# Second pair of a two-phase kernel: subtractions and operand loads placed elsewhere in the chains, part of them on another engine

## The chip, the cores and the metric

One core of one Trainium2 chip runs the whole program. The metric is device time in microseconds (us) of one execution, and a kernel's time is the median of its runs. The engines are named as the profile names them: PE (TensorE, matmuls) with PEld (its weight loads), DVE (VectorE), ACT (ScalarE), POOL (GpSimd) and SP (SyncE, which issues all DMAs here). Each engine works through its own instructions strictly in the order written; semaphores tie the engines together.

## The reference

```python
def reference(**kwargs):          # attention, then two MLPs, 4608 tokens
    attn_out = _attn_ref(...)     # linear attention, 8 x 8 x 576 x 64
    x = ...                       # 4608 x 512
    x = _moe_ref(x, w_in, w_out)              # (h * cos(h)) @ w_out, h = x @ w_in
    return _moe2_ref(x, w1, w2, w3, w_out)

def _moe2_ref(x, w1, w2, w3, w_out):          # w1, w2: 512 x 1024, w3: 1024 x 1024
    a = x @ w1
    b = x @ w2
    h = a * b @ w3
    return (h @ w_out).astype(np.float32)
```

The change touches only the last function, here called the second pair.

## The kernel before

The program first does the attention and the first MLP, and writes the second MLP's input x2, transposed, to device memory. It also multiplies w3 by w_out once (the tensor w_c), so that the second pair is a, b = x2 w1, x2 w2 (phase one) and o = (a*b) w_c (phase two). Each product of fp32 matrices is done as three matmuls of a high and a low part: ACT copies the rounded high part (line 122), DVE or POOL subtracts it to get the low part (line 124). All three products use a recursive 2 x 2 scheme with seven products of sums of blocks in place of eight, so every operand is needed in seven combinations (0 to 6), which take further subtractions.

**Phase one** runs over twelve pairs (h, g): h is a half of w1 and w2, g one of six groups of 768 tokens. A pair has four chains (`Chain`, `at` = 0 to 3), and a chain has seven products of six matmuls of 384 columns. The order on PE is `open1` (product 1 into bank X, product 2 into bank Y), `close1` of the chain before (its product 4), `open2` (product 6 into X), `close2` of the chain before (its product 3), `open3` (product 5 into V, product 7 into X). Call these the slots 1 to 7 of a chain. By the table `PAIR` they read the token operands `xc` 0, 1, 6 (of the chain before), 4, 2 (of the chain before), 3 and 5. ACT copies X out three times per chain (line 1396) before PE may add to X again; chains with `at` 0 and 2 make a, those with 1 and 3 make b, and `done` multiplies (line 1447) and `quarter` (lines 1364 to 1372) makes four subtractions and additions per product a*b. The seven resulting combinations of a*b go to device memory (line 1345).

**The token operands** of the next group come from `xc_steps` (line 1301): one tile `x2r` (tag "x", a single buffer) is loaded by four DMAs; then seven ACT copies, seven low-part subtractions and four subtractions of blocks (lines 1319, 1321, 1322, 1328) make xc 0, 1, 4, 3, 5, 2, 6 in that order. Eight buffers of tag "xc" hold seven operands, so a new operand takes the place of one whose last product has been read. All eleven subtractions run on POOL, while POOL also makes `quarter` from the seventh pair on (line 1594). Where in the chains a step is written is set by tables in `second` (lines 1558 to 1588): (pair, chain, place), with places o1, c1, o2, c2, o3 after open1, close1, and so on. `w12_steps` (line 1165) and `wc_stages` (line 1274) are placed in the same way; `wc_stages` makes the operands `wq` of w_c in the last pairs, in two halves h, all its subtractions on POOL.

**Phase two** (`Out`) runs over eighteen pairs of 2 x 128 tokens: seven products of twelve matmuls of 256 columns each. Its left operands are the seven stored combinations of a*b, loaded by `load_left` in three DMAs (of 3, 3 and 1 combinations) and split by `split_left` on ACT and DVE. The loads of pair n+2 are written at the end of pair n, and pair n+1 is split during pair n.

Of the kernel before, what the change touches and what calls it, by code (L numbers as in the profile page):

```python
# [33 lines left out]
def kernel(  # L34
# [1418 lines left out]
    def load_left(n, i):  # L1453
        if n < len(PAIRS):
            g, s = PAIRS[n]
            k = len(COMBOS[i])
# [79 lines left out]
    def second(last_set):  # L1536
# [27 lines left out]
        for dp, i, at in (  # L1564
            (0, 0, ((0, 3, "o1"), (1, 0, "o3"), (1, 1, "o1"), (1, 1, "o2"), (1, 2, "o1"),
                    (1, 2, "c1"))),
            (0, 1, ((1, 3, "o1"), (2, 0, "o3"), (2, 1, "o1"), (2, 1, "o2"), (2, 1, "o3"),
                    (2, 2, "o1"))),
            (1, 0, ((2, 0, "o3"), (2, 2, "o2"), (2, 2, "o3"), (2, 3, "o1"), (2, 3, "o2"),
                    (2, 3, "o3"))),  # L1570
            (1, 1, ((2, 1, "o1"), (3, 0, "o1"), (3, 0, "o2"), (3, 0, "o3"), (3, 1, "o1"),
                    (3, 1, "o2"))),
# [12 lines left out]
        on((k, 3, "c1"), load_left, 0, 1)
        on((k, 3, "c1"), load_left, 0, 2)
        on((k, 3, "o3"), split_left, 0, 1)
        on((k, 3, "o3"), split_left, 0, 2)
# [316 lines left out]
```

## Time and profile before

| | us |
|---|---|
| median of 3 runs | 1472.31 (1470.74 to 1475.21) |
| the profiled execution | 1474.78 |
| its span, first to last instruction | 1473.0 |
| PE busy | 1418.3 (96%) |
| DVE busy | 947.5 (64%) |
| ACT busy | 718.5 (49%) |
| POOL busy | 641.1 (44%) |

The profile is one execution, 1.8 us longer than its span. A share of busy time is an average over stages; matmuls overlap, so a busy PE can still run slowly. What a stage loses is read from the starts of its matmuls: their number times the pace of an undisturbed stretch, against the time that passed. The granted clock of a stretch is given as a share of 2.4 GHz.

### The profile page before, as it was taken

How to read it: one execution, taken by the hardware profiler on the slowest of the kernel's cores; microseconds unless marked ns; L12 is line 12 of the kernel's file. 1: busy time of each engine (PE TensorE's matmuls, PEld its weight loads, DVE VectorE, ACT ScalarE, POOL GpSimd, SP SyncE). 2: the span in 40 equal slices, each digit the busy share in tenths (PEclk: the TensorE clock that was granted, in tenths of full speed). 3: DMA queues.
4: the chain of work that ended last, by engine and by line, in shares of the span. 5: the costliest groups of instructions: out<-in, count | busy, mean ns of one | idle time of the engine just before them, and what ended most of it. 6: DMA issues, size and time to landing. Idle time of an engine off the chain costs nothing.

```text
span 1473.0 us, 23476 instructions
## 1 busy us (share of the span) xinstructions
PE 1418.3 (96%) x8376; PEld 1246.3 (85%) x8376; DVE 947.5 (64%) x1500; ACT 718.5 (49%) x1365; POOL 641.1 (44%) x522
## 2 busy tenths in 40 slices
PE   7999999999999999999999999999999889899998
PEld 5877777777777889988888879999999889899998
DVE  5786566674878667888888675666653333555553
ACT  5665655555556555555555354433333233445453
POOL 1174664485554622122223197845665476600000
PEclk9999999999999999999999999999999999999999
DMA  9385996797689988999999844445424243566654
GB/s 340 124 283 143 317 287 208 246 324 243 197 301 342 351 326 310 323 322 359 345 358 368 290 167 139 144 129 158 140 87 124 75 133 124 175 236 230 249 202 164
DMA packets 210837, 345.56 MB, mean 235 GB/s; under 512 B 19136, under 2 KB 120608, under 8 KB 210464
## 3 DMA queue, kind: packets, MB, share of 16 engines
q1 hardware_dynamic: 210016, 343.48, 68.1%
q8 instruction: 65, 1.06, 0.3%
q10 hardware_dynamic: 704, 0.59, 0.1%
q14 instruction: 52, 0.43, 0.1%
HBM read 205.89 MB, written 138.11 MB: 234 GB/s over the span
## 4 chain that ended last, share of the span: by engine, by line
PE 61%; DMA 13%; POOL 9%; DVE 6%; issue 5%; ACT 3%; SPq 2%; POOLq 0%; ACTq 0%; DVEq 0%
PE X L1080 13%; PE X L1388 10%; PE V L1080 7%; PE h L906 5%; DMA ab_raw<-ab 5%; PE h L907 5%; PE h L908 5%; PE V L1388 4%; PE Y L1080 3%; PE Y L1388 3%; POOL xc L124 2%; ACT ab_hl L122 2%; PE oX L1483 2%; DVE ab_hl L124 1%; DMA bc<-rsd 1%
## 5 line engine op out<-in xcount | busy, mean ns | idle before, releaser
L1388 PE MATMUL X<-xc,w 128*128 128x384 f32 x1152 | 226.7, 344 | 24.0 <-POOL xc L124 20.5
L906 PE MATMUL h<-x,w_in 128*128 128x512 f32 x576 | 230.6, 400 | 3.9 <-DVE u L1699 3.9
L1388 PEld LDWEIGHTS X<-xc,w 128*128 128x128 f32 x1152 | 208.4, 194 | 27.6 <-POOL xc L124 23.0
L907 PE MATMUL h<-x,w_in 128*128 128x512 f32 x576 | 225.6, 392 | 2.0 <-DVE x L124 2.0
L908 PE MATMUL h<-x,w_in 128*128 128x512 f32 x576 | 225.2, 391 | 0.0
L1080 PE MATMUL X<-g_hl,wl 128*128 128x512 f32 (+1 forms) x960 | 199.8, 368 | 0.0
L1080 PEld LDWEIGHTS X<-g_hl,wl 128*128 128x128 f32 x960 | 167.3, 189 | 30.3 <-DVE wl L124 0.2
L124 POOL TENSOR_TENSOR g_hl<-g_raw,g_hl 128x1024 fp32r<-128x1024 f32 x29 | 74.2, 2558 | 232.5 <-ACT g_hl L122 158.7
L1725 DVE SCALAR_TENSOR_TENSOR u<-h,r 128x512 f32<-128x512 f32 x136 | 93.4, 687 | 113.7 <-ACT r L1724 92.2
L124 DVE TENSOR_TENSOR g_hl<-g_raw,g_hl 128x1024 fp32r<-128x1024 f32 x97 | 136.8, 1437 | 38.5 <-ACT g_hl L122 38.1
L1396 ACT ACTIVATE s<-X 128x384 f32<-128x384 f32 x144 | 70.7, 491 | 185.4 <-PE X L1388 185.4
L122 ACT ACTIVATE g_hl<-g_raw 128x1024 fp32r<-128x1024 f32 x126 | 130.5, 1057 | 60.9 <-DMA g_raw<-g 58.6
L1724 ACT ACTIVATE r<-h 128x512 int32<-128x512 f32 x136 | 81.5, 599 | 128.4 <-PE h L908 125.6
L906 PEld LDWEIGHTS h<-x,w_in 128*128 128x128 f32 x576 | 108.5, 188 | 41.1 <-DVE u L1699 8.1
L907 PEld LDWEIGHTS h<-x,w_in 128*128 128x128 f32 x576 | 108.5, 188 | 24.7 <-DVE x L124 3.2
L908 PEld LDWEIGHTS h<-x,w_in 128*128 128x128 f32 x576 | 108.5, 188 | 23.1
L1483 PE MATMUL oX<-wq,ab_hl 128*128 128x256 f32 x864 | 112.1, 286 | 6.8 <-ACT os L1493 6.8
L124 DVE TENSOR_TENSOR ab_hl<-ab_raw,ab_hl 128x512 fp32r<-128x512 f32 x126 | 84.3, 716 | 50.4 <-ACT ab_hl L122 49.4
L1483 PEld LDWEIGHTS oX<-wq,ab_hl 128*128 128x128 f32 x864 | 107.8, 194 | 8.3 <-ACT os L1493 8.1
L1388 PE MATMUL V<-xc,w 128*128 128x384 f32 x576 | 108.6, 336 | 0.0
L124 POOL TENSOR_TENSOR xc<-x2r,xc 128x768 fp32r<-128x768 f32 x49 | 93.7, 1936 | 30.9 <-ACT xc L122 30.9
L1388 PEld LDWEIGHTS V<-xc,w 128*128 128x128 f32 x576 | 101.3, 189 | 0.0
(194 smaller groups left out, 2456.5 us busy)
## 6 DMA issues: line engine op xcount, KB each, us to landing
g_raw<-g SPq DMA_DIRECT2D x126, 512.0 KB
ab_raw<-ab SPq DMA_DIRECT2D x36, 768.0 KB
ab<-q SPq DMA_DIRECT2D x96, 192.0 KB
kvraw<-in_kv_main_dram SPq DMA_DIRECT2D x32, 512.0 KB
g<-ta SPq DMA_DIRECT2D x32, 512.0 KB
g<-tb SPq DMA_DIRECT2D x32, 512.0 KB
g<-u SPq DMA_DIRECT2D x28, 512.0 KB
ab<-s SPq DMA_DIRECT2D x72, 192.0 KB
```

The costliest lines, as they stand in the source:

```text
L122: hi = nc.scalar.activation(dst[:, 0], src, AF.Copy)
L124: lo = lo_engine.tensor_tensor(dst[:, 1], src, f32(dst[:, 0]), ALU.subtract)
L906: nc.tensor.matmul(ps, w[0], x[0], start=first, stop=False)
L907: nc.tensor.matmul(ps, w[0], x[1], start=False, stop=False)
L908: return nc.tensor.matmul(ps, w[1], x[0], start=False, stop=last).ins
L1080: nc.tensor.matmul(ps, w[:, a, i2, ws], g[:, b, q], start=first and half == 0 and q == 0 and n == 0, stop=last and final and q == KH - 1 a ...
L1388: nc.tensor.matmul(ps, w[:, self.i, a, k], x[:, b, k], start=first and k == 0 and n == 0, stop=last and k == 1 and n == 2, skip_group_chec ...
L1396: nc.scalar.activation(s, ps, AF.Copy)
L1483: nc.tensor.matmul(ps, t[:, a, k], w[:, b], start=first and k == 0 and n == 0, stop=last and k == 3 and n == 2, skip_group_check=True,)
L1724: nc.scalar.activation(r, h_ps[n], AF.Identity, bias=0.25, scale=INV_2PI)
L1725: nc.vector.scalar_tensor_tensor(u, h_ps[n], INV_2PI, r, ALU.mult, ALU.subtract)
```

## The change

All of it is in the second pair.

- `xc_steps`: the places of the seven stages move earlier: the load of x2r from o3 of chain 1 to o3 of chain 0, the last two stages from c1 and o2 of the next pair to o3 of chain 3 and c1 of the next pair. The last of its four block subtractions goes from POOL to DVE.
- `w12_steps` of the second half of w1 and w2: places moved to fit, no instruction added.
- `quarter`: always on DVE (from the seventh pair on it was on POOL). That is 48 subtractions of 128x384.
- `wc_stages`: the four block subtractions of each half on DVE in place of POOL, the low parts still on POOL, in six stages in place of five and in another order.
- `load_left`: pair 0 by one DMA of all seven combinations into the tile "x"; pair 1 at o1 of the last chain of phase one; pair n+2 at the beginning of pair n in place of its end. `split_left` of pair 0 is spread over the last two chains.

```diff
@@ wc_stages
         s(0, b11)
+        yield
         adder.tensor_tensor(b11, b12, b11, SUB)
-        yield
         adder.tensor_tensor(b12, b22, b12, SUB)
         s(2, b22)
         yield
+        s(3, b11)
+        s(5, b12)
         adder.tensor_tensor(b22, b22, b11, SUB)
+        yield
         s(1, b21)
-        s(3, b11)
+        s(4, b22)
         yield
-        s(4, b22)
         adder.tensor_tensor(b21, b21, b22, SUB)
         yield
-        s(5, b12)
         s(6, b21)
@@ xc_steps
-        adder.tensor_tensor(b21, b21, t2, SUB)
+        vec.tensor_tensor(b21, b21, t2, SUB)
@@ load_left
+        if n == 0:
+            t = m1.tile([P, 7, 4, P], F32, tag="x", name="ab_raw_0")
+            nc.sync.dma_start(out=t, in_=ab_d[g][:, s])
...
@@ second
-            at = [(k, 1, "o3"), (k, 2, "o2"), (k, 2, "o3"), (k, 3, "o2"), (k, 3, "o3"),
-                  (k + 1, 0, "c1"), (k + 1, 0, "o2")]
+            at = [(k, 1, "o2"), (k, 2, "o1"), (k, 3, "o1"), (k, 3, "c2"), (k, 3, "o3"),
+                  (k + 1, 0, "c1")]
+            at[:0] = [(k, 0, "o3")]
...
-        stages(lambda: wc_stages(1, pool, pool), (
+        stages(lambda: wc_stages(1, vec, pool), (
...
-        on((k, 1, "o1"), load_left, 0, 0)
+        on((k, 1, "o3"), load_left, 0)
...
+        on((k, 3, "o1"), load_left, 1)
...
-                c.adder = vec if k < 6 else pool
+                c.adder = vec
...
             c.open1()
+            load_left(n + 2)
             split_left(n + 1, 0)
...
             split_left(n + 1, 2)
-            for i in range(3):
-                load_left(n + 2, i)
```

On POOL, around the passage from pair (1, 3) to pair (0, 4), where `xc` of group 4 is made. Before:

```order
L124 TENSOR_TENSOR xc_1_11100<-x2r_10983,xc_1_11100 128x768
L124 TENSOR_TENSOR xc_4_11103<-x2r_10983,xc_4_11103 128x768
L124 TENSOR_TENSOR xc_3_11131<-x2r_10983,xc_3_11131 128x768
L1328 TENSOR_TENSOR x2r_10983<-x2r_10983 128x768
L1364 TENSOR_TENSOR s_11162<-q_1311_11129,q_1311_11160 128x384
L1365 TENSOR_TENSOR q_1311_11160<-q_1311_11160,q_1311_11081 128x384
L1366 TENSOR_TENSOR s_11162<-q_1311_11160,q_1311_11129 128x384
L124 TENSOR_TENSOR xc_5_11166<-x2r_10983,xc_5_11166 128x768
L124 TENSOR_TENSOR xc_2_11169<-x2r_10983,xc_2_11169 128x768
L124 TENSOR_TENSOR xc_6_11180<-x2r_10983,xc_6_11180 128x768
```

The same place on POOL now:

```order
L124 TENSOR_TENSOR xc_1_11083<-x2r_10920,xc_1_11083 128x768
L124 TENSOR_TENSOR xc_4_11086<-x2r_10920,xc_4_11086 128x768
L124 TENSOR_TENSOR xc_3_11113<-x2r_10920,xc_3_11113 128x768
L124 TENSOR_TENSOR xc_5_11135<-x2r_10920,xc_5_11135 128x768
L124 TENSOR_TENSOR xc_2_11138<-x2r_10920,xc_2_11138 128x768
L124 TENSOR_TENSOR xc_6_11172<-x2r_10920,xc_6_11172 128x768
```

The block subtraction (L1328) and the three of `quarter` have left the queue between xc 3 and xc 5.

On ACT, in the last pair: s is a copy of bank X (s_1501 of chain 1, s_1510 of chain 2, s_1511 of chain 3), wq the operands of w_c (second half), ab_hl the left operands of pair 0. Before:

```order
L1396 ACTIVATE s_1510_12183<-X_12141 128x384
L1396 ACTIVATE s_1510_12211<-X_12141 128x384
L122 ACTIVATE ab_hl_0_12214<-ab_raw_0_12085 128x512
L122 ACTIVATE ab_hl_1_12217<-ab_raw_0_12085 128x512
L122 ACTIVATE ab_hl_4_12220<-ab_raw_0_12085 128x512
L1396 ACTIVATE s_1511_12232<-X_12225 128x384
```

And now, from the first half of the block to the same copy of chain 3:

```order
L1397 ACTIVATE s_1501_12136<-X_12061 128x384
L122 ACTIVATE wq_6_12141<-wc_raw 128x512
L1397 ACTIVATE s_1510_12154<-X_12147 128x384
L1397 ACTIVATE s_1510_12183<-X_12147 128x384
L1397 ACTIVATE s_1510_12211<-X_12147 128x384
L122 ACTIVATE ab_hl_0_12214<-ab_raw_12144 128x512
L122 ACTIVATE ab_hl_1_12217<-ab_raw_12144 128x512
L122 ACTIVATE ab_hl_4_12220<-ab_raw_12144 128x512
L1397 ACTIVATE s_1511_12232<-X_12225 128x384
```

The three copies of ab_hl stand ahead of the first copy of chain 3 in both; the tile that they read is another one, and its DMA stands elsewhere in SP's queue.

On SP, at the same place (ab is device memory; q and s are products and sums of a*b on their way to it). Before:

```order
L1458 DMA ab_raw_0_12085<-ab_90 128x1536
L1345 DMA ab_93<-q_1501_12079 384x1x128
...
L1345 DMA ab_93<-q_1511_12242 384x1x128
L1458 DMA ab_raw_1_12253<-ab_90 128x1536
L1458 DMA ab_raw_2_12255<-ab_90 128x512
L1345 DMA ab_93<-q_1511_12288 384x1x128
L1458 DMA ab_raw_0_12303<-ab_90 128x1536
```

And now:

```order
L1460 DMA ab_raw_12144<-ab_90 128x3584
L1346 DMA ab_93<-q_1501_12139 384x1x128
L1346 DMA ab_93<-s_12173 384x1x128
...
L1346 DMA ab_93<-s_12173 384x1x128
L1467 DMA ab_raw_0_12253<-ab_90 128x1536
L1467 DMA ab_raw_3_12255<-ab_90 128x1536
L1467 DMA ab_raw_6_12257<-ab_90 128x512
L1346 DMA ab_93<-q_1511_12242 384x1x128
```

Pair 0 is one DMA behind the product q_1501 of chain 1, and pair 1 (ab_raw_0, 3, 6) stands ahead of the products of chain 3.

## Rows read from the trace of the kernel before

**Rows 1.** Windows of lines 1388, 1483: length, PE, PEld busy (count), clock, DMA, GB/s.

```profile
885.10:1274.30 389.20, 362.35 (x2004) 357.95 (x2004) 0.96 0.41 126
1274.30:1469.60 195.30, 185.62 (x1512) 184.13 (x1512) 0.98 0.61 220
```

**Rows 2.** Waits of PE: who, for whom, us in total, times, longest.

```profile
PE X L1388 <- POOL xc L124: 20.5, 8, 4.8
PE oX L1483 <- ACT os L1493: 6.8, 6, 2.9
...
PE X L1388 <- ACT s L1396: 3.5, 3, 1.6
PE Y L1388 <- POOL xc L124: 2.8, 2, 1.4
```

**Rows 3.** Timeline: start, length, engine, line, operation, tiles, count, [idle before].

```profile
1146.21 5.36 POOL L124 TENSOR_TENSOR xc<-x2r,xc 128x768 fp32r<-128x768 f32 x3
...
1148.07 3.89 PE L1388 MATMUL X<-xc,w 128*128 128x384 f32 x11 [4.76 <-POOL xc L124]
...
1153.38 2.24 PE L1388 MATMUL X<-xc,w 128*128 128x384 f32 x12
...
1155.46 2.24 PE L1388 MATMUL V<-xc,w 128*128 128x384 f32 x12
```

**Rows 4.** Windows: PE, PEld, DVE, ACT, POOL busy, clock, DMA share, GB/s.

```profile
1148.00:1152.00 4.00, 3.93 (x12) 3.93 (x13) 0.56 (x1) 0.50 (x2) 4.00 (x4) 0.50 0.21 61
1153.40:1163.00 9.60, 9.60 (x57) 9.60 (x56) 3.92 (x7) 2.03 (x5) 0.41 (x1) 1.00 0.20 61
```

**Rows 5.** Lines by form, 885 to 1285: count, busy us, mean ns, idle before.

```profile
L124 POOL TENSOR_TENSOR xc<-x2r,xc 128x768 fp32r<-128x768 f32 x49 | 93.7, 1936 | 30.9 <-ACT xc L122 30.9
...
L122 ACT ACTIVATE xc<-x2r 128x768 fp32r<-128x768 f32 x49 | 39.9, 841 | 13.1 <-POOL x2r L1328 11.5 <-POOL x2r L1321 1.6
...
L1447 DVE TENSOR_TENSOR q<-Y,a 128x384 f32<-128x384 f32 x48 | 26.8, 557 | 2.9
...
L124 POOL TENSOR_TENSOR wq<-wc_raw,wq 128x512 fp32r<-128x512 f32 x14 | 17.8, 1289 | 0.3 <-ACT wq L122 0.3
...
L1366 DVE TENSOR_TENSOR s<-q,q 128x384 f32<-128x384 f32 x12 | 14.1, 1178 | 0.4
...
L122 ACT ACTIVATE wq<-wc_raw 128x512 fp32r<-128x512 f32 x14 | 8.7, 627 | 11.5 <-POOL wc_raw L1294 6.9 <-POOL wc_raw L1289 3.0 <-POOL wc_raw L1284 1.7
```

**Rows 6.** Timeline, last pair of phase one.

```profile
1264.85 0.63 ACT L122 ACTIVATE wq<-wc_raw 128x512 fp32r<-128x512 f32 x1 [3.42 <-POOL wc_raw L1294]
1265.38 0.47 ACT L1396 ACTIVATE s<-X 128x384 f32<-128x384 f32 x1
1265.91 2.36 PE L1388 MATMUL X<-xc,w 128*128 128x384 f32 x12 [1.55 <-ACT s L1396]
```

**Rows 7.** Timeline, passage from phase one to phase two.

```profile
1278.80 2.19 ACT L122 ACTIVATE ab_hl<-ab_raw 128x512 fp32r<-128x512 f32 x4 [3.76 <-DMA ab_raw<-ab]
...
1281.31 1.83 PE L1483 MATMUL oX<-wq,ab_hl 128*128 128x256 f32 x12 [2.88 <-ACT os L1493]
```

**Rows 8.** Timeline, phase two: a load, the copies that wait for it, matmuls.

```profile
1312.17 1.39 SPq L1458 DMA_DIRECT2D ab_raw<-ab  x3
...
1316.63 1.67 ACT L122 ACTIVATE ab_hl<-ab_raw 128x512 fp32r<-128x512 f32 x3 [2.52 <-DMA ab_raw<-ab]
...
1410.21 1.67 ACT L122 ACTIVATE ab_hl<-ab_raw 128x512 fp32r<-128x512 f32 x3 [5.39 <-DMA ab_raw<-ab]
...
1416.89 3.04 PE L1483 MATMUL oX<-wq,ab_hl 128*128 128x256 f32 x24
1419.77 3.04 PE L1483 MATMUL oV<-wq,ab_hl 128*128 128x256 f32 x24
...
1466.41 1.69 PE L1483 MATMUL oX<-wq,ab_hl 128*128 128x256 f32 x12 [0.47 <-ACT os L1493]
```

**Rows 9.** Windows while left operands load, columns as in Rows 4.

```profile
1278.00:1282.00 4.00, 1.12 (x8) 0.80 (x7) 2.54 (x5) 2.62 (x6) 0.00 (x0) 1.00 1.05 412
```

More of the change, by code (lines that the diff above doesn't have):

```diff
@@ L1451, with load_left @@
     COMBOS = ((0, 1, 4), (3, 5, 2), (6,))
[L1453 to L1456, printed above, removed]
+    def load_left(n):
+        if n >= len(PAIRS):
+            return
+        g, s = PAIRS[n]
+        if n == 0:
+            t = m1.tile([P, 7, 4, P], F32, tag="x", name="ab_raw_0")
+            nc.sync.dma_start(out=t, in_=ab_d[g][:, s])
+            raw_of[n] = [t[:, i] for i in range(7)]
+            return
+        raw_of[n] = []
+        for i in range(0, 7, 3):
+            k = min(3, 7 - i)
             t = pr.tile([P, k, 4, P], F32, tag="xc", bufs=8, name=f"ab_raw_{n}_{i}")
-            nc.sync.dma_start(out=t, in_=ab_d[g][:, s, 3 * i:3 * i + k])
-            raw_of[n, i] = t
+            nc.sync.dma_start(out=t, in_=ab_d[g][:, s, i:i + k])
+            raw_of[n] += [t[:, j] for j in range(k)]
     def split_left(n, i):
         if n < len(PAIRS):
-            raw = raw_of.pop((n, i))
-            for k, c in enumerate(COMBOS[i]):
+            for c in COMBOS[i]:
                 t = w_home(14 + 7 * (n % 2) + c, [P, 2, 4, P], F32R, f"ab_hl_{n}_{c}")
-                split(t, raw[:, k], vec)
+                split(t, raw_of[n][SLOT[c]], vec)
                 left_of[n, c] = t
@@ L1560, in second @@
                 continue
-            at = [(k, 1, "o3"), (k, 2, "o2"), (k, 2, "o3"), (k, 3, "o2"), (k, 3, "o3"),
-                  (k + 1, 0, "c1"), (k + 1, 0, "o2")]
+            at = [(k, 1, "o2"), (k, 2, "o1"), (k, 3, "o1"), (k, 3, "c2"), (k, 3, "o3"),
+                  (k + 1, 0, "c1")]
+            at[:0] = [(k, 0, "o3")]
+            if k == 3:
+                at[:3] = [(k, 1, "o2"), (k, 2, "o1"), (k, 2, "o3")]
             stages(lambda g=order[k + 1][1]: xc_steps(g, pool), at)
         for dp, i, at in (
-            (0, 0, ((0, 3, "o1"), (1, 0, "o3"), (1, 1, "o1"), (1, 1, "o2"), (1, 2, "o1"),
-                    (1, 2, "c1"))),
+            (0, 0, ((0, 3, "o1"), (1, 1, "c1"), (1, 1, "o3"), (1, 2, "o2"), (1, 2, "o3"),
+                    (1, 3, "c1"))),
             (0, 1, ((1, 3, "o1"), (2, 0, "o3"), (2, 1, "o1"), (2, 1, "o2"), (2, 1, "o3"),
                     (2, 2, "o1"))),
[L1569 to L1572, printed above, removed]
+            (1, 0, ((2, 0, "o3"), (2, 2, "c1"), (2, 2, "o2"), (2, 2, "o3"), (2, 3, "o1"),
+                    (2, 3, "o2"))),
+            (1, 1, ((2, 0, "o3"), (2, 3, "c2"), (2, 3, "o3"), (3, 0, "o2"), (3, 0, "o3"),
+                    (3, 1, "o1"))),
         ):
@@ L1576, in second @@
         on((k - 1, 1, "o3"), wc_load)
-        stages(lambda: wc_stages(0, pool, pool), (
-            (k - 1, 2, "o3"), (k - 1, 3, "o1"), (k - 1, 3, "o2"), (k - 1, 3, "o3"), (k, 0, "o1")
-        ))
-        stages(lambda: wc_stages(1, pool, pool), (
-            (k, 0, "o3"), (k, 1, "o1"), (k, 1, "o2"), (k, 1, "o3"), (k, 2, "o1")
+        stages(lambda: wc_stages(0, vec, pool), (
+            (k - 1, 2, "o3"), (k - 1, 3, "o1"), (k - 1, 3, "o2"), (k - 1, 3, "o3"), (k, 0, "o1"),
+            (k, 0, "o2"),
+        ))
+        stages(lambda: wc_stages(1, vec, pool), (
+            (k, 0, "o3"), (k, 1, "o1"), (k, 1, "c1"), (k, 1, "o2"), (k, 1, "c2"), (k, 1, "o3"),
         ))
-        on((k, 1, "o1"), load_left, 0, 0)
+        on((k, 1, "o3"), load_left, 0)
         on((k, 2, "o3"), split_left, 0, 0)
[L1585 to L1588, printed above, removed]
+        on((k, 3, "o1"), split_left, 0, 1)
+        on((k, 3, "o1"), load_left, 1)
+        on((k, 3, "o2"), split_left, 0, 2)
         n, prev = 0, None
@@ L1624, in second @@
             split_left(n + 1, 2)
-            for i in range(3):
-                load_left(n + 2, i)
             prev = c
```

1 line of the change is left out of this document (removed).

## The prediction, made before the changed kernel was run

> **What bounds the kernel now.** I read the windows of the two phases first [rows 1]. Until the first matmul of o, phase one issues 2004 matmuls in 389.2 us. Undisturbed they run at 0.173 us each: twelve start at 1153.38 and the next twelve at 1155.46 [rows 3]. That makes 347.3 us, so phase one loses 41.9. Phase two issues 1512 at 0.120 us (24 between 1416.89 and 1419.77 [rows 8]) and the last twelve of phase one, 183.5 us together, in 195.3; it loses 11.8. PE bounds both phases, and **53.7 us** is all that the change can win, since nothing ahead of 885 us is altered.
>
> The waits of PE [rows 2] say where the loss is. Ten waits for the low parts of xc on POOL make 20.5 + 2.8 = 23.3 us, three for the copy s on ACT 3.5 us, and six in phase two, for the copy os on ACT, 6.8 us. That is 33.6; the other 20 are what follows a wait. The largest wait shows it [rows 3, 4]: after 4.76 us of idleness the 17 matmuls from 1148.07 to 1153.38 take 5.31 us where 2.95 is the pace, and the granted clock of that stretch is 0.50 (1.2 GHz), against 1.00 a little later. I give the s waits 4.3 us with their restarts, which leaves 41.9 - 4.3 = 37.6 for the xc waits, so 14.3 beyond the ten waits themselves: **1.4 us per wait on the average**.
>
> Then I looked at what the releasing engine had been doing. At the largest wait, POOL runs three low parts of xc in a row from 1146.21 [rows 3], and PE starts when the first is done. POOL is late because its queue is full there: eleven operations of about 1.94 us [rows 5], 21.3 us, with three of quarter between them, begun too late for the chains that need them. In the last pair, ACT waits 3.42 us for a block subtraction on POOL, its copy of X comes behind that, and PE waits 1.55 [rows 6]. In phase two ACT waits for the loads of the left operands: 3.76 us, whereupon PE idles 2.88 [rows 7], and 5.39 late in the phase [rows 8].
>
> **xc: 37.6 lost, 1.5 kept.** Take the last chain ahead of a new group, slot 1 at 0, seven slots of 1.04, so the next chain begins at 7.28 and the one after at 14.56. A product's result is there 1.2 us after its start (twelve matmuls span 2.24 [rows 3]). ACT's copies of X take 0.47 [rows 6], those of xc 0.84 [rows 5]. Written where they now are, xc 1 is copied by 2.6, xc 4 by 3.4, xc 3 by 5.8, xc 5 by 8.8, xc 2 by 9.7; xc 6 waits until its buffer is free (slot 3 of the next chain) and is copied by 11.4. POOL at 1.94 has xc 1 at 4.5, xc 4 at 6.5, xc 3 at 8.4, xc 5 at 10.8, xc 2 at 12.7, xc 6 at 14.6. PE needs them at 8.3, 10.4, 12.5, 13.5, 18.7 and 16.6. Every one is at least 2.0 us early, so all ten waits should go. xc 0 and the other block subtractions lie a chain or more ahead. The load is free of cost as long as x2r, which is one buffer, is released: POOL frees it at 14.6, SP stands at the load until then with no product queued behind it that is ready, and the first row block is wanted by ACT about 5 us later; the first of three loads needs 4.5 (issue 1312.17, copy 1316.63 [rows 8]). What could remain: in the first two groups POOL also has the half-size low parts of w, which eat the 2 us; I keep 1.0 for both. ACT now has two copies of xc ahead of the next chain's first copy of X: by the same arithmetic that one ends at 10.2, and PE adds to X from 10.4, so I keep 0.5 for seven groups (bounds 0 and 3.5, half a microsecond each).
>
> **Subtractions on DVE: 0.** 48 of quarter, 7 of x2r and 8 of wc come to DVE. A product with an operand in PSUM takes 0.557 there, a subtraction with both operands in SBUF 1.178 in the mean, in the stretches where POOL works beside it [rows 5]. Per two chains (14.56 us) DVE has ten operations of 0.557 and four to five of 1.18, 10.3 to 11.5 us; at 1.94 each, the length of the POOL operation, 15.3. PE waits for DVE nowhere in either phase now [rows 2], though quarter is on DVE in the first six pairs already. So the cost is 0; the lower bound is 0 as well, the upper (15.3 - 14.56) x 7 = 5 us. The Trainium skill has a rule against this edit (SBUF — State Buffer, "Who interferes with whom"): a VectorE instruction with two SBUF inputs and a GpSimd instruction that reads SBUF block each other for a whole instruction. The longer mean of the row agrees; by the rule the time would lie nearer to the upper bound.
>
> **wc: 4.3 lost, 1.0 kept.** Let u be slot 1 of chain 1 of the last pair. ACT has copied block b11 by u+1.3 and POOL its low part by 2.7 (1.289 each [rows 5]); DVE, behind the two operations of Y, does b11 and b12 by u+5.0, b22 by 6.3; ACT copies wq 3 and 5 by 5.65, then X by 6.1 (PE wants it at 6.24). POOL works off wq 2, 3, 5, 1 by u+8.9; only then may DVE overwrite b21 (1.29 at the worst, 10.2), ACT copies wq 6 by 10.85 and chain 2's X by 11.3, where PE wanted it at 10.4. That is a wait of about 1 us in place of three; the half of w_c ahead of it has more room. Bounds 0 and 3.
>
> **Passage to phase two: 4.9 lost, 4.2 kept.** The load of pair 0 now goes into tile "x", in which w_c lies. POOL's last low part ends at u+12.2, so SP issues at about u+12.3, though the place in the code is u+7.3. It brings 128 x 3584 x 4 = 1.835 MB. The first of three DMAs, 0.786 MB, needs 4.46 from issue to copy [rows 8]; the other 1.05 MB at the 412 GB/s of a loaded stretch [rows 9] 2.55 more: 7.0, landing at u+19.3. ACT stands at the copies of ab_hl from u+16.2, in the queue ahead of the first X copy of the last chain. Three copies take 1.67 [rows 8], X 0.47: u+21.5. PE, already 1.0 late, wants it at u+18.7. So PE waits 2.8, and with 1.4 for the restart loses **4.2**. What it loses there now is of the same size: 2.88 idle [rows 7], and about 2.0 with the restart, 4.9. So this edit wins almost nothing: the wait for the load moves from the first product of o into the last chain. Bounds 0.5 (load landing at u+16) and 7 (the 5.39 [rows 8] says that a load can be 2 to 3 us later). The Trainium skill advises one DMA in place of several, as the edit has it, and 358 GB/s for transfers from device memory (SBUF — State Buffer, "Summary: rules for kernel authors"); by that figure the second part takes an estimated 2.9 us and PE waits 0.4 longer, while the trace has 412.
>
> **Rest of phase two: 6.9 lost, 0.7 kept.** The other os waits (6.8 - 2.88) and their restarts come from loads issued only at the end of the pair before. With loads at the beginning of pair n for pair n+2, ACT has a whole pair, 7 x 12 x 0.120 = 10.1 us, more than the 4.5 to 7 that a load takes. The wait in the last pair, 0.47 with its refill 0.7 [rows 8], is for PE's own X and stays.
>
> **Sum.** 53.7 - (1.5 + 0 + 1.0 + 4.2 + 0.7) = 46.3 won. The profiled execution took 1474.78 (span 1473.0 and 1.8 around it): 1428.5. It lies 2.5 over the median of the runs, so I say **1428**.
>
> **Rivals.** (a) The load of pair 0 lands in time, because POOL or DVE finish w_c earlier than I reckon: 4.2 less, **1424**. For it: several of my steps are upper ends. Against: 1.835 MB can't land in under 4.5 us at 412 GB/s. (b) The xc waits move and don't go: SP stands at the load of x2r in consecutive groups, everything of xc is 2 to 3 us later than in my table, and PE still waits once in each of the seven groups, 1.9 + 1.4 each: 23 us, **1450**. For it: the largest xc wait falls where POOL is fullest, and one x2r buffer serves load and subtraction. Against: 2 us of room, and POOL has four fewer operations there. (c) Loads are not a pair ahead in fact, since buffers of tag "xc", or products of a*b not yet ready ahead of them in SP's queue, hold SP back; the 6.2 won in phase two shrinks to nothing: **1434**. (d) Slower: DVE. Quarter, b21 and the PSUM operations share one queue, and when DVE falls behind by more than the spare of its two chains, banks V and Y come free late and PE stands. At m us for each of five SBUF operations, DVE needs 5.6 + 5 m in 14.56: it decides from m = 1.8 on, and eats all 46 at 7 groups from m = 3.1. At 3.5 it is 8.5 x 7 = 60 us: **1488**. Against: the mean is 1.178 with POOL busy beside it [rows 5].
>
> **How the numbers follow.** Chances: forecast 0.66, (a) 0.12, (b) 0.13, (c) 0.06, (d) 0.03. The range takes the forecast with its bounds (kept terms of 1 to 18 us, the upper ends hardly all at once), (a) and (c), and part of (b): 1420 to 1445. What a measurement of this kernel can tell from no change is about 0.3%, 4.4 us. Faster by more than that: all but (d) and some unforeseen cost, 0.94; within 0.02; slower 0.04.
>
> **What would show it.** Right: PE's list of waits has no POOL xc line, or under 3 us; a wait for s behind ab_hl in the last chain, with ACT standing at ab_raw for about 3 us; no ab_raw wait of ACT that reaches PE in phase two; phase one about 354 us long to the first matmul of o, phase two about 184. Wrong: POOL xc still among the longest waits (b), os waits spread over phase two (c), or PE waiting for Y, V or X on DVE (d).

## The result, and the profile after

The changed kernel takes **1429.65 us** (median of 4 runs, 1428.91 to 1430.37) against 1471.92 before; the ratio is 0.9709 (95% interval 0.9692 to 0.9726), so it is faster by 42.3 us. I had said 1428, in a range from 1420 to 1445. The profiled execution took 1428.91 (span 1426.2), where my sum, made against the profiled execution of before, gave 1428.5. That they meet this closely is partly luck, as the next lines show.

Both phases of the changed kernel in windows; the columns are those of [rows 1] with DVE, ACT and POOL between PEld and the clock:

```profile
880.60:1238.10 357.50, 351.22 (x2005) 348.67 (x2005) 252.53 (x368) 141.14 (x274) 190.19 (x124) 1.00 0.48 146
1238.10:1422.60 184.50, 183.97 (x1526) 183.57 (x1524) 100.25 (x182) 90.23 (x192) 0.00 (x0) 1.00 0.60 216
```

Phase one is 357.5 us long, 389.2 before [rows 1]; I had said about 354. Phase two is 184.5, 195.3 before; I had said 184. Together they are 42.5 shorter, where I had reckoned with 46.3. What made up for it is the time ahead of the second pair: the first matmul of phase one starts at 880.65 here and at 885.16 in the trace of before, though nothing ahead of it was changed. In the profiles of the twelve runs below it starts between 883.2 and 891.4. So differences of a few microseconds are read below from **the stretch**, from the first matmul of phase one to the last of phase two: 584.4 before, 541.9 now.

The waits of PE in that stretch (who, for whom, total, times, longest), to be set beside [rows 2]:

```profile
PE X L1389 <- ACT s L1397: 6.1, 4, 3.3
PE oX L1491 <- ACT os L1501: 0.5, 1, 0.5
```

No POOL xc line is left, and of six os waits only the one in the last pair. The new line numbers are L1389 for L1388, L1397 for L1396, L1491 for L1483, L1501 for L1493. What these waits cost with the restarts behind them I take from the starts of successive matmuls, as whatever goes beyond 0.174 us in phase one and 0.120 in phase two. It was 53.0 us; now it is 10.7, in four places:

| place | lost before | predicted to stay | lost now |
|---|---|---|---|
| xc, and w ahead of the chains | 37.1 | 1.5 | 2.2 |
| w_c in the last pair | 4.3 | 1.0 | 2.7 |
| passage to phase two | 4.7 | 4.2 | 5.1 |
| rest of phase two | 6.9 | 0.7 | 0.7 |

The places of xc work as in the table of the prediction. In one of the groups POOL does the six low parts in one row, and here PE waits for none of them (timeline: start, length, engine, line, operation, tiles, count, idle before):

```profile
1105.51 2.24 PE L1389 MATMUL X<-xc,w 128*128 128x384 f32 x12
...
1109.09 12.00 POOL L124 TENSOR_TENSOR xc<-x2r,xc 128x768 fp32r<-128x768 f32 x6 [3.57 <-ACT xc L122]
```

The twelve matmuls of the first row are slot 7 of one chain and slot 1 of the next, which so lies at 1106.55. POOL ends at 1121.09, so xc 6 is ready 14.5 us behind slot 1; I had said 14.6, with 16.6 as the time at which PE wants it. POOL waits 3.57 us for ACT ahead of them: it is early now.

The last pair, with u (slot 1 of chain 1) at 1208.47:

```profile
1214.34 5.47 POOL L124 TENSOR_TENSOR wq<-wc_raw,wq 128x512 fp32r<-128x512 f32 x4 [1.72 <-ACT wq L122]
...
1218.59 1.77 DVE L1296 TENSOR_TENSOR wc_raw<-wc_raw 128x512 f32<-128x512 f32 x1 [1.96 <-POOL wq L124]
...
1220.39 0.63 ACT L122 ACTIVATE wq<-wc_raw 128x512 fp32r<-128x512 f32 x1 [3.13 <-DVE wc_raw L1296]
...
1221.45 1.33 PE L1389 MATMUL X<-xc,w 128*128 128x384 f32 x6 [1.60 <-ACT s L1397]
...
1222.41 0.33 SPq L1460 DMA_DIRECT2D ab_raw<-ab  x1
...
1230.22 1.67 ACT L122 ACTIVATE ab_hl<-ab_raw 128x512 fp32r<-128x512 f32 x3 [3.78 <-DMA ab_raw<-ab]
...
1231.79 0.47 ACT L1397 ACTIVATE s<-X 128x384 f32<-128x384 f32 x1
...
1232.31 1.70 PE L1389 MATMUL X<-xc,w 128*128 128x384 f32 x6 [3.29 <-ACT s L1397]
```

These are the two chains that the prediction worked out: DVE's last subtraction stands until POOL has read block b21, ACT's copy of X stands behind the split of its result, and PE waits 1.60. Then ACT stands 3.78 us at the load of pair 0, with a copy of X in the queue behind, and PE waits 3.29.

### The profile page after: what moved, and what is told of

Read it like the earlier page. It is cut to its first block, busy times and chain, and to the rows that moved or that the text cites. A ratio compares the mean times of both kernels' runs of the same rounds, so it can differ in the third digit from the quotient of the medians.

```text
span 1426.2 us, 23445 instructions
## 1 busy us (share of the span) xinstructions
PE 1403.2 (98%) x8376; PEld 1234.5 (87%) x8376; DVE 1006.9 (71%) x1563; ACT 720.7 (51%) x1365; POOL 579.0 (41%) x459
## 4 chain that ended last, share of the span: by engine, by line
PE 89%; DMA 4%; DVE 3%; POOL 1%; issue 1%; SPq 1%; ACT 1%; POOLq 0%; DVEq 0%; ACTq 0%
PE X L1080 14%; PE X L1389 13%; PE h L906 8%; PE oX L1491 7%; PE h L907 7%; PE h L908 7%; PE V L1080 7%; PE V L1389 7%; PE oV L1491 4%; PE Y L1080 3%; PE Y L1389 3%; PE oY L1491 2%; DMA g<-u 1%; PE wc L908 1%; PE wc L907 1%; PE wc L906 1%
## 5 line engine op out<-in xcount | busy, mean ns | idle before, releaser
L1389 PE MATMUL X<-xc,w 128*128 128x384 f32 x1152 | 216.9, 335 | 6.1 <-ACT s L1397 6.1
L1389 PEld LDWEIGHTS X<-xc,w 128*128 128x128 f32 x1152 | 201.1, 188 | 7.8 <-ACT s L1397 7.7
L1397 ACT ACTIVATE s<-X 128x384 f32<-128x384 f32 x144 | 70.7, 491 | 171.8 <-PE X L1389 169.0
L124 POOL TENSOR_TENSOR xc<-x2r,xc 128x768 fp32r<-128x768 f32 x49 | 97.1, 2009 | 102.6 <-ACT xc L122 102.3
L1491 PE MATMUL oX<-wq,ab_hl 128*128 128x256 f32 x864 | 109.9, 283 | 0.5 <-ACT os L1501 0.5
L1389 PE MATMUL V<-xc,w 128*128 128x384 f32 x576 | 109.4, 337 | 0.1
L1491 PEld LDWEIGHTS oX<-wq,ab_hl 128*128 128x128 f32 x864 | 106.5, 192 | 0.7 <-ACT os L1501 0.7
L1389 PEld LDWEIGHTS V<-xc,w 128*128 128x128 f32 x576 | 101.8, 190 | 1.1 <-DVE a L1441 1.1
L124 DVE TENSOR_TENSOR ab_hl<-ab_raw,ab_hl 128x512 fp32r<-128x512 f32 x126 | 80.5, 685 | 30.4 <-ACT ab_hl L122 28.9
```

What stands on the lines that cost most here:

```text
L124: lo = lo_engine.tensor_tensor(dst[:, 1], src, f32(dst[:, 0]), ALU.subtract)
L1389: nc.tensor.matmul(ps, w[:, self.i, a, k], x[:, b, k], start=first and k == 0 and n == 0, stop=last and k == 1 and n == 2, skip_group_chec ...
L1397: nc.scalar.activation(s, ps, AF.Copy)
L1491: nc.tensor.matmul(ps, t[:, a, k], w[:, b], start=first and k == 0 and n == 0, stop=last and k == 3 and n == 2, skip_group_check=True,)
```

## The experiments

The runs stand in three groups, e1 to e4, e5 to e8 and e9 to e12; the kernel before, run beside each, had medians of 1473.73, 1474.36 and 1472.87 us. "Stretch" and "lost" are from the profile of each run, medians from its timed runs.

| kernel | median us | ratio to before, 95% | stretch us | lost us |
|---|---|---|---|---|
| before | 1471.92 | | 584.4 | 53.0 |
| changed | 1429.65 | 0.9692 to 0.9726 | 541.9 | 10.7 |
| e12 changed, again | 1434.75 | 0.9722 to 0.9762 | 540.0 | 8.8 |
| e1 old places of xc | 1456.96 | 0.9853 to 0.9938 | 567.6 | 36.1 |
| e2 old quarter | 1438.31 | 0.9719 to 0.9799 | 545.0 | 13.8 |
| e3 w_c on POOL | 1435.39 | 0.9704 to 0.9791 | 544.6 | 13.3 |
| e4 old loads of o | 1435.78 | 0.9704 to 0.9782 | 546.3 | 15.1 |
| e5 new places alone | 1441.24 | 0.9748 to 0.9794 | 551.7 | 20.6 |
| e6 three of xc late | 1433.22 | 0.9695 to 0.9740 | 544.5 | 13.3 |
| e7 load of pair 0 free | 1426.89 | 0.9649 to 0.9698 | 536.8 | 5.6 |
| e8 three more on DVE | 1474.41 | 0.9988 to 1.0016 | 582.1 | 50.7 |
| e9 e7 with late w_c | 1425.13 | 0.9660 to 0.9689 | 534.3 | 3.2 |
| e10 one more on DVE | 1446.30 | 0.9810 to 0.9845 | 550.7 | 19.5 |
| e11 three more, spread | 1456.97 | 0.9876 to 0.9905 | 566.9 | 35.3 |

**The base, e12.** The changed kernel as it is.

> The changed kernel once more, beside the others on this chip, as the base for differences of a few us. Nothing is undone: 1428 to 1433 is expected.

It came out at 1434.75, above what was expected; its stretch is 540.0, and what is longer lies ahead of it (first matmul of phase one at 888.9). So a median here says nothing below some 5 us. The stretch leaves out that part of the time, but it is read from one execution of each kernel, and the two of the changed kernel differ by 1.9 us, nearly all of it in the last chain (5.1 and 3.2 lost). A difference of 2 to 5 us in the stretch is therefore read only together with the wait that makes it.

### One part undone, one part alone

**e1**: the places of x2's work as before, and b21 on POOL.

```
-        vec.tensor_tensor(b21, b21, t2, SUB)
+        adder.tensor_tensor(b21, b21, t2, SUB)
...
-            at = [(k, 1, "o2"), (k, 2, "o1"), (k, 3, "o1"), (k, 3, "c2"), (k, 3, "o3"),
-                  (k + 1, 0, "c1")]
-            at[:0] = [(k, 0, "o3")]
...
+            at = [(k, 1, "o3"), (k, 2, "o2"), (k, 2, "o3"), (k, 3, "o2"), (k, 3, "o3"),
+                  (k + 1, 0, "c1"), (k + 1, 0, "o2")]
```

> The changed kernel with the token operands undone: the places of the stages of xc_steps as before and the last block subtraction of x2r on POOL again; quarter, w_c and the loads of o stay changed. Theory (the places in the chains make the low parts early enough): the waits of PE for POOL xc come back. In the kernel before they cost 37.6 us, but in its two largest (groups 4 and 5) three operations of quarter stood in POOL's queue, which are now on DVE; without them I expect these two to shrink to the size of the others (3.8 us each): 25 to 30 us more than the changed kernel, 1455 to 1460. Rival (quarter on DVE alone frees POOL enough): under 8 us more, below 1438.

1456.96, as the theory had it. PE's waits:

```profile
PE X L1389 <- POOL xc L124: 16.2, 12, 2.3
PE X L1389 <- ACT s L1397: 5.2, 3, 3.0
PE Y L1389 <- POOL xc L124: 2.3, 1, 2.3
```

Thirteen xc waits are back, and the stretch is 25.7 longer. This run undoes two things, the places and b21 on DVE; no run separates them.

**e2**: quarter on POOL from the seventh pair on.

```
-                c.adder = vec
+                c.adder = vec if k < 6 else pool
```

> The changed kernel with quarter on POOL again from the seventh pair on, the rest changed. Theory: POOL has two or more us of room, quarter now stands behind xc 5 and xc 2 but ahead of xc 6 in two groups (3.1 us of work, room 2.0), and beside w_c in the last pair: 2 to 5 us more, 1432 to 1435. Rival (moving quarter is what won): 15 us or more on top, over 1444. Rival (VectorE is hurt by it): the time falls below 1428.

The median (1438.31) lies between the two; the stretch is 3.1 longer, as the theory has it. Two short waits for xc are back, 1.6 us together and 2.1 lost at them:

```profile
PE X L1389 <- ACT s L1397: 6.9, 4, 3.0
PE X L1389 <- POOL xc L124: 1.6, 2, 0.9
```

**e3**: the eight block subtractions of w_c on POOL, at the new places.

```
-        stages(lambda: wc_stages(0, vec, pool), (
+        stages(lambda: wc_stages(0, pool, pool), (
...
-        stages(lambda: wc_stages(1, vec, pool), (
+        stages(lambda: wc_stages(1, pool, pool), (
```

> The changed kernel with the eight block subtractions of w_c on POOL again, in the new order and places. Theory: POOL's row for the second half grows by four operations of 1.29 us, its last low part ends 3 to 5 us later, with it the load of pair 0, and ACT waits for POOL again ahead of its copies of X: 5 to 9 us more, 1435 to 1439. Rival (w_c hides beside the chains wherever it runs): within 2 us of the changed kernel.

1435.39. The stretch is 2.7 longer, of which 1.3 is a single wait of V for DVE in an earlier chain and 1.4 lies in the last pair. The median can't tell this from e12. So the theory, with 5 to 9, had too much: in the last pair, where most of these subtractions stand, having them on DVE is worth 1.4 us, nearer to the rival.

**e4**: loads and splits of the left operands as before.

```
-            t = m1.tile([P, 7, 4, P], F32, tag="x", name="ab_raw_0")
-            nc.sync.dma_start(out=t, in_=ab_d[g][:, s])
...
-        on((k, 1, "o3"), load_left, 0)
+        on((k, 1, "o1"), load_left, 0, 0)
...
-            load_left(n + 2)
...
+            for i in range(3):
+                load_left(n + 2, i)
```

> The changed kernel with the loads and splits of the left operands of o as before (three DMAs for pair 0, the first at chain 1, pairs loaded at the end of the pair ahead). Theory: the 6.2 us of phase two come back, while the passage costs about the same in both versions (4.9 before, 5.1 measured in the changed kernel): 5 to 7 us more, 1435 to 1437. Rival (the load of pair 0 into the tile of w_c is a loss that eats the gain): within 2 us. Rival (the loads are worth more, since they also disturb phase one): over 10 us more.

1435.78; the median can't tell this from e12. The stretch is 4.4 longer, a little less than the theory had. The wait in the last chain of phase one is gone, and os waits are back in phase two:

```profile
PE oX L1484 <- ACT os L1494: 5.6, 4, 4.1
PE X L1389 <- ACT s L1397: 3.0, 3, 1.6
```

The theory took the passage to cost the same in both. It doesn't: the passage loses 1.5 here, where the changed kernel loses 5.1, and the rest of phase two 7.3, where the changed kernel loses 0.7. Of these 7.3, 6.6 lie at one place, behind the longest wait (4.1). So with the other parts of the change in place, the new load of pair 0 is a loss of 3.6, and what pays is that the later pairs are loaded earlier.

**e5**: the kernel before with the new places of x2's and w1/w2's steps, and b21 on DVE.

```
-        adder.tensor_tensor(b21, b21, t2, SUB)
+        vec.tensor_tensor(b21, b21, t2, SUB)
...
-            at = [(k, 1, "o3"), (k, 2, "o2"), (k, 2, "o3"), (k, 3, "o2"), (k, 3, "o3"),
-                  (k + 1, 0, "c1"), (k + 1, 0, "o2")]
+            at = [(k, 1, "o2"), (k, 2, "o1"), (k, 3, "o1"), (k, 3, "c2"), (k, 3, "o3"),
+                  (k + 1, 0, "c1")]
+            at[:0] = [(k, 0, "o3")]
...
```

> The kernel before with one part of the change alone: the new places of x2's rows, subtractions and splits (b21 on VectorE), and the new places of the w1/w2 splits. Quarter stays on POOL from the seventh pair on, w_c and the loads of o as before. Theory: the places carry the gain of xc. In the trace of before, the second pair loses 53.0 us, of it 37.1 at xc waits. With the new places and quarter on POOL the trace of e2 loses 2.1 at xc waits and 1.7 at the copy behind the w1/w2 subtractions. So this kernel should lose 53.0 - 37.1 + 3.8 = 19.7, that is 33 less than before: 1437 to 1442, with two short xc waits and the s and os waits of before. Rival: the places work only because quarter has left POOL. Undoing the places cost 25 us and not 37, so 12 belong to quarter, and this kernel would come out at 1447 to 1450, with an xc wait in most groups.

1441.24, and 20.6 lost where the theory said 19.7. PE's waits:

```profile
PE oX L1483 <- ACT os L1493: 6.3, 6, 3.2
PE X L1388 <- ACT s L1396: 4.1, 4, 1.6
PE X L1388 <- POOL xc L124: 1.7, 2, 1.0
```

The places, with b21, bring 32.7 of the 42.5 us by themselves. Undone alone they cost 25.7: with quarter off POOL, the old places lose less. The two places where quarter stood between the low parts lost 9.0 and 9.4 us before, and lose 3.2 each in e1. Both parts relieve the same queue, and the 7 us between the two numbers are won by either.

### The spare of xc

**e6**: xc 5, 2 and 6 back at their late places.

```
-            at = [(k, 1, "o2"), (k, 2, "o1"), (k, 3, "o1"), (k, 3, "c2"), (k, 3, "o3"),
-                  (k + 1, 0, "c1")]
+            at = [(k, 1, "o2"), (k, 2, "o1"), (k, 3, "o1"), (k, 3, "c2"), (k + 1, 0, "c1"),
+                  (k + 1, 0, "o2")]
```

> The changed kernel with the last three low parts of xc (5, 2 and 6) put back to the places that they have in the kernel before, the other four staying early. In the table of the prediction xc 5 would be ready at 12.9 where PE wants it at 13.5, and in the trace of the changed kernel POOL's six low parts in a row end 14.5 us after slot 1, as the table has it. Theory (the table): no xc wait or a very short one in each group: 0 to 4 us more than the changed kernel, 1430 to 1434. Rival (b): the spare is less than reckoned, and one wait of 1.9 with 1.4 for the restart comes back in each of seven groups: 1452, with seven POOL xc waits of PE.

1433.22, and no xc wait at all; rival (b) falls. POOL now does three low parts, idles, and does three:

```profile
1116.89 6.17 POOL L124 TENSOR_TENSOR xc<-x2r,xc 128x768 fp32r<-128x768 f32 x3 [3.57 <-ACT xc L122]
...
1124.17 6.10 POOL L124 TENSOR_TENSOR xc<-x2r,xc 128x768 fp32r<-128x768 f32 x3 [1.11 <-ACT xc L122]
```

With b21 off POOL, it is enough that the first four are early; the late three were late before because POOL came to them late. The 2.6 us by which the stretch is longer are two waits of V for DVE (1.0 each, `PE V L1389 <- DVE a L1441` in its waits).

### The passage and w_c

**e7**: the load of pair 0 in two parts, the first of them early and in a buffer that is free.

```
+            if part == 0:
+                t = pr.tile([P, 3, 4, P], F32, tag="xc", bufs=8, name="ab_raw_0_0")
+                nc.sync.dma_start(out=t, in_=ab_d[g][:, s, 0:3])
...
-        on((k, 1, "o3"), load_left, 0)
+        on((k, 0, "o3"), load_left, 0)
+        on((k, 1, "o3"), load_left, 0, 1)
...
-        on((k, 3, "o1"), split_left, 0, 1)
...
+        on((k, 3, "o2"), split_left, 0, 1)
+        on((k, 3, "o3"), split_left, 0, 2)
```

> The changed kernel with the load of pair 0 in two: the three combinations that ACT splits in the last chain go early into a free buffer of the tag xc, the other four into tile x as before, and the second and third split stand one place later. Theory: ACT stood 3.78 us at this load, and the copy of X behind it cost PE 3.29 of waiting and 5.1 in all. With the load out of the way ACT reaches the copy of X in time, the passage loses 0 to 1, and the kernel is 4 to 5 us shorter than the changed one: 1424 to 1427. Rival: ACT is held by the low parts of w_c, not by the load, and the wait stays where it is: no difference, 1428 to 1432.

1426.89; the stretch is 5.1 shorter than the changed kernel's, 3.2 shorter than that of e12, and in both cases this is the whole loss of the passage there. The load was the cause, and not the splits of w_c ahead of it, whose 2.7 us are still lost. That the first part is smaller, is issued earlier and has a free buffer comes in one edit; which of the three would do by itself isn't shown. First part, copies, and the second part's copies, with no wait:

```profile
1215.37 0.57 SPq L1462 DMA_DIRECT2D ab_raw<-ab  x1
...
1232.27 1.67 ACT L122 ACTIVATE ab_hl<-ab_raw 128x512 fp32r<-128x512 f32 x3
...
1236.49 1.66 ACT L122 ACTIVATE ab_hl<-ab_raw 128x512 fp32r<-128x512 f32 x3
```

**e9**: e7, and the stages of the second half of w_c one to two slots later.

```
-            (k, 0, "o3"), (k, 1, "o1"), (k, 1, "c1"), (k, 1, "o2"), (k, 1, "c2"), (k, 1, "o3"),
+            (k, 0, "o3"), (k, 1, "o1"), (k, 1, "o2"), (k, 1, "o3"), (k, 2, "o1"), (k, 2, "o2"),
...
+        on((k, 2, "o2"), load_left, 0, 1)
```

> e7 (the load of pair 0 in two) and, with it, the stages of the second half of w_c at later places: their last two in the third chain of the last pair. In the trace of e7, 1.87 and 0.81 us are still lost at two copies of X that stand on ACT behind the splits of w_c. Theory: with the later places ACT no longer waits for VectorE's last subtraction of w_c ahead of an X copy, and most of these 2.7 us go; the second part of the load follows tile x, which comes free two to four us later, and still lands ahead of its split. 1 to 3 us less than e7: 1424 to 1426. Rival: the waits move into the third chain with the stages, and the time is that of e7, 1426 to 1428.

1425.13, and 3.2 lost in all. In the last pair DVE's subtraction still runs, but the copies of X stand ahead of the split that waits for it:

```profile
1224.72 1.76 DVE L1296 TENSOR_TENSOR wc_raw<-wc_raw 128x512 f32<-128x512 f32 x1
...
1226.26 0.49 ACT L1397 ACTIVATE s<-X 128x384 f32<-128x384 f32 x1 [2.31 <-PE X L1389]
1226.65 0.62 ACT L122 ACTIVATE wq<-wc_raw 128x512 fp32r<-128x512 f32 x1
```

Its interval against before (0.9660 to 0.9689) lies under that of the changed kernel beside it (0.9722 to 0.9762), so this version beats both kernels.

### The spare of DVE

**e8**: three more subtractions per two chains ahead of those of quarter (three behind q2, one behind q1).

```
+            for _ in range(3):
+                adder.tensor_tensor(sums[:, 2], x[3], t, SUB)
             adder.tensor_tensor(sums[:, 1], x[3], t, SUB)
```

> The changed kernel with three more subtractions of 128x384 per two chains on VectorE, ahead of the four of quarter; they write a tile that is overwritten, so nothing else changes. It measures the spare of VectorE (rival (d)). In the changed kernel's trace the ten operations with PSUM take 0.557 and the five with SBUF operands 1.0 to 1.4 each, 10.6 to 11 of 14.56 us. Three more of 0.7 to 1.4 make it 12.7 to 15. Theory: what counts is the sum over two chains; under 14.56 it costs little: 0 to 8 us more, up to 1438. Rival: what counts is the burst, since the seven stand in a row ahead of the next operation that frees a bank of PE; each pair of chains then loses 1 to 2 us, 24 pairs 25 to 50 us: 1455 to 1480.

1474.41: 72 subtractions of 1.1 us eat the whole gain. Waits of PE, and phase one in windows:

```profile
PE V L1391 <- DVE a L1443: 25.1, 14, 7.0
```

```profile
884.50:1282.20 397.70, 363.94 (x2005) 357.61 (x2004) 303.65 (x437) 140.68 (x274) 188.10 (x124) 0.96 0.43 131
```

DVE is busy 303.65 of 397.70 us, 76%, and yet PE waits for it. The time is that of the rival. One place in the timeline shows how PE comes to wait:

```profile
1042.62 4.38 DVE L1366 TENSOR_TENSOR s<-q,q 128x384 f32<-128x384 f32 x3 [0.93 <-DMA ab<-q]
...
1046.92 0.55 DVE L1367 TENSOR_TENSOR s<-q,q 128x384 f32<-128x384 f32 x1
...
1047.63 4.20 POOL L124 TENSOR_TENSOR xc<-x2r,xc 128x768 fp32r<-128x768 f32 x2 [1.65 <-ACT xc L122]
1048.10 2.07 DVE L1369 TENSOR_TENSOR s<-q,q 128x384 f32<-128x384 f32 x1
...
1052.17 0.55 DVE L1443 TENSOR_TENSOR a<-V,s 128x384 f32<-128x384 f32 x1
...
1052.77 4.21 PE L1391 MATMUL V<-xc,w 128*128 128x384 f32 x12 [3.36 <-DVE a L1443]
```

The six subtractions and the three operations behind them run from 1042.62 to 1052.17, and only then does DVE read bank V, for which PE waits. Subtractions of the same size, 128x384, take 0.55 us with POOL idle (1046.92) and 2.07 us beside its low parts (1048.10).

That it is the burst alone, and not the sum, e8 doesn't show, since the sums are not alike. Call the time from the beginning of one row behind q2 to the next a period; it is 14.56 us long where PE doesn't wait. Three of them (columns as in the windows above):

```profile
1003.27:1026.37 23.10, 16.12 (x86) 15.80 (x85) 19.11 (x19) 7.60 (x13) 16.14 (x9) 0.85 0.29 94
1062.46:1077.84 15.38, 14.88 (x86) 14.56 (x85) 11.76 (x17) 4.43 (x9) 6.73 (x4) 1.00 0.63 185
1112.65:1127.21 14.56, 14.56 (x86) 14.56 (x85) 9.24 (x18) 3.45 (x7) 0.00 (x0) 1.00 0.32 96
```

With POOL idle, 18 operations of DVE take 9.24 us, and PE loses nothing. Beside POOL 19 of them take 19.11, more than the 14.56 that a period has, and behind this row stands the longest wait of V, 7.0:

```profile
1007.04 2.04 POOL L1322 TENSOR_TENSOR x2r<-x2r 128x768 f32<-128x768 f32 x1
...
1011.64 2.04 DVE L1368 TENSOR_TENSOR q<-q,q 128x384 f32<-128x384 f32 x1
```

There one subtraction of DVE takes as long as one instruction of POOL. The four longest waits (3.1 to 7.0) all lie in periods in which DVE is busy for 14.6 us or more, so there the sum is too long as well. In the middle period DVE is busy 11.76, and PE still waits 0.5: there the sum can't be the reason, and the order of the row is. No wait of V lies behind any of the seven rows beside which POOL is idle.

**e10**: one more in place of three.

```
+            adder.tensor_tensor(sums[:, 2], x[3], t, SUB)
             adder.tensor_tensor(sums[:, 1], x[3], t, SUB)
```

> As e8, with one more subtraction per two chains in place of three, at the same place ahead of the four of quarter. e8 lost 40 us for 72 of 1.1 us, all of it where V waits for VectorE. Theory (no spare in the burst): what each adds comes out at PE at once, a third of e8: 10 to 16 us more than the changed kernel, 1440 to 1447. Rival (a threshold): there is room for one, and PE sees little of it: 0 to 6 us more, 1429 to 1436.

1446.30, as the theory had it. The profile is of the shortest of the four runs (1439.71) and shows somewhat less than the median, 8.8 lost beyond the changed kernel's 10.7, of it five waits of V:

```profile
PE V L1390 <- DVE a L1442: 7.4, 5, 2.5
```

So not every subtraction comes out at PE: in this execution 19 of the 24 rows take theirs without a wait, and five, all beside a busy POOL, do not. The two longest waits (1.9 and 2.5) lie in periods in which DVE is busy for more than 14.56 us; the other three, of 1.0, in periods with 13.4 to 14.2, such as this one, so there the order of the row counts:

```profile
1026.02:1041.10 15.08, 14.08 (x81) 13.76 (x81) 13.44 (x16) 7.27 (x13) 11.41 (x7) 1.00 0.31 94
```

**e11**: three more, one behind each of q0, q3 and q1.

```
         if q == 0:
...
+            x["s"] = sums = pr.tile([P, 3, H], F32, tag="st", name="s_%d%d%d" % key)
+            adder.tensor_tensor(sums[:, 2], t, t, SUB)
         elif q == 3:
...
+            adder.tensor_tensor(x["s"][:, 2], t, x[0], SUB)
...
```

> As e8, the same number of further subtractions of 128x384 on VectorE, 72 in all, but spread: one behind each of the products q0, q3 and q1, none in the row of quarter behind q2. Theory (the burst decides): VectorE has idle time between the other products, so that each is absorbed there: 0 to 12 us more than the changed kernel, 1429 to 1442. Rival (the sum over two chains decides): as slow as e8, 1465 to 1480.

1456.97, between the two expectations, and it settles less than I wanted. The tile of the sums is now taken earlier, and DVE stands 42.9 us waiting until the DMAs have read it (group of DVE in phase one: busy, mean ns, idle before):

```profile
L1362 DVE TENSOR_TENSOR s<-q 128x384 f32<-128x384 f32 x24 | 22.1, 922 | 43.0 <-DMA ab<-s 42.9
```

That wait is my edit's own and nothing of the burst. Even with it the stretch is 15.2 shorter than that of e8, so the order of the row makes about that much of e8's loss at least; how much the spread work by itself would cost stays open.

## Why the prediction was right, point by point

**What bounds.** PE bounds both phases and only its losses could be won: right. The losses fell by 42.3 us in the two profiles, and the medians by 42.3.

**xc, 37.6 lost, 1.5 kept.** Right: 37.1 were lost and 2.2 are, none of it for POOL's low parts of xc. The 2.2 are of another kind than those I kept 1.0 and 0.5 for. For 1.5 of them DVE's subtractions for w1 and w2, not POOL's low parts, come late in the second of the twelve pairs, and ACT's copy of X stands behind their split:

```profile
931.64 0.95 DVE L1189 TENSOR_TENSOR w12raw<-w12raw 128x256 f32<-128x256 f32 x1
...
932.62 0.42 ACT L122 ACTIVATE w<-w12raw 128x256 fp32r<-128x256 f32 x1 [2.38 <-DVE w12raw L1189]
...
933.47 1.32 PE L1389 MATMUL X<-xc,w 128*128 128x384 f32 x6 [0.64 <-ACT s L1397]
```

DVE is late there because the three subtractions of quarter just ahead, at 927.44, take 4.2 us beside POOL; in e1, where POOL is idle at that place, the same three take 1.7, and there is no such wait. The change put POOL's work beside them, and neither this term nor the next had that. Why the new places work is shown by e1 (undone, 25.7 more), e5 (alone, 32.7 less) and e6 (the early four suffice), always for the places together with b21 on DVE.

**Subtractions on DVE, 0.** Right in the number, at least for the waits of V, of which there is none; the spare that I gave as the reason isn't there. I summed over two chains with a mean length: 10.3 to 11.5 of 14.56, so 3 to 4 us to spare. The periods of the changed kernel are not alike, neither in the sum nor in the length of one subtraction (windows of two of them, columns as above):

```profile
927.44:942.32 14.88, 14.16 (x79) 13.21 (x78) 13.52 (x18) 7.89 (x15) 13.69 (x10) 1.00 0.43 129
1074.06:1088.62 14.56, 14.56 (x86) 14.56 (x85) 7.74 (x14) 3.44 (x7) 0.00 (x0) 1.00 0.32 95
```

Where POOL is idle, DVE needs 7.74; in the fullest period ahead of the last pair it needs 13.52, and about 1 us is left. The 1.178 of [rows 5] is a mean over both kinds of row: in the trace of before three subtractions in a row take 1.7 us at 997.10, with POOL idle, and 5.3 at 916.27, with POOL busy throughout. e10 agrees: one more subtraction of about 1.1 us costs 9 us in its profile and some 12 in the median beside e12. In e3, e4 and e6 a wait of V of 1.0 shows once or twice even without it. So that no wait of V came was near the edge, and rival (d) was nearer than its 0.03, which rested on that mean. On the length of one subtraction the rows meet the rule: the Trainium skill (SBUF — State Buffer, "Who interferes with whom") says that a VectorE instruction with two SBUF inputs and a GpSimd instruction that reads SBUF exclude each other. The trace of e8 agrees, 2.07 beside POOL's low part at 1047.63 against 0.55 with POOL idle.

**w_c, 1.0 kept; 2.7 measured.** The mechanism was right, its size off. I had DVE begin b21 at u+8.9; it did at u+10.1, since POOL began the row of four low parts at u+5.9, later than in my table, and took 5.47 for them in place of 4 x 1.289 = 5.16. Then the subtraction took 1.77, for which I had 1.29 as the worst. That is 1.60 of waiting in place of 1.0. The other 0.8 is a wait of 0.54 at 1215.41, one copy of X earlier, where my table had 0.14 us of room.

**Passage, 4.2 kept; 5.1 measured.** Issue at u+13.9 (I said 12.3, and the whole difference comes from w_c, ahead of it), use 7.8 us after the issue (I said 7.0). In these 7.8 us all transfers together move at 272 GB/s, not at the 412 of [rows 9] with which I priced the second part:

```profile
1222.40:1230.20 7.80, 6.63 (x39) 6.31 (x37) 3.99 (x8) 0.98 (x2) 0.00 (x0) 1.00 0.87 272
```

The figure of the Trainium skill that I weighed (SBUF — State Buffer, "Summary: rules for kernel authors", 358 GB/s) would have given an estimated 7.4 us from issue to use, nearer than mine and still below the 7.8; products of a*b are written in the same time, and what they cost the load isn't shown. That the edit wins nothing at this place held, 4.7 before and 5.1 now; e7 shows that the load makes it, and e4 that the old load would lose only 1.5 here by now.

**Rest of phase two, 0.7 kept.** Right to the tenth; e4 brings the os waits back. Rival (c) doesn't occur.

**The sum.** The parts kept 10.7, where I said 7.4; the profiled executions differ by 4.5 us ahead of the change, in my favour. Without that the sum would have missed its execution by some 5 us (1433.4 for 1428.5). I ought to have allowed for such a difference: it is larger than any one of the terms that I kept.

## What to carry to other kernels

When an engine's queue is the late one, spread its work over the time in which the data is already there, and see that what is first needed is first done; taking operations away from it wins in part the same microseconds (here 7 of them). The spare of the engine that takes the work over is not its share of busy time, nor a mean over the stage: with DVE 71% busy PE had no wait of V for it, with 76% the stretch was 40 us longer. Look at the fullest period, at the lengths that the operations have there beside the other engine (0.56 or 2.0 us here for the same subtraction), and at the row ahead of the next operation that frees a bank. A copy that PE waits for must not stand behind a split whose data is on its way; moving the load of one such split into a buffer that was free was worth 5.1 us here, moving the stages of the second half of w_c by a slot or two 2.4.
